# Raw rows from another queue, a schedule dated step by step, and 12 probability buffers

## The chip, the cores and the metric

The kernel runs on one core of a Trainium2 chip. The metric is the device time of one execution in microseconds (us), as the median of several runs. The engines are named as in the profile: PE (TensorE, matrix products; PEld is its loading of weights), ACT (ScalarE), DVE (VectorE), POOL (GpSimd) and SP (SyncE, which here only issues DMAs; SPq and POOLq are the issuing queues of SP and POOL).

## The reference

```python
# q, k, v: (4 batches, 8 heads, 768 rows, 64);  centroids: (8, 16, 64)
q_assign = argmax(einsum('bhsd,hcd->bhsc', q_n, c_n))     # q_n, k_n, c_n: rows over their lengths
k_assign = argmax(einsum('bhsd,hcd->bhsc', k_n, c_n))
scores = matmul(q, k.T) / sqrt(64), -1e9 where q_assign != k_assign
attn = softmax(scores);  x = (attn @ v) as (3072 tokens, 512)
h = x @ w_in                                              # w_in: 512 x 2048
out = (h * sigmoid(h)) @ w_out                            # w_out: 2048 x 512
```

A query attends only to the keys that fall to the same centroid; a gated layer of width 2048 follows.

## The kernel before

**The stages of one head.** A head is one of 32 pairs (batch, head), numbered 0 to 31; batch 1 begins at head 8, batch 2 at 16, batch 3 at 24. Its raw rows of q and k (`raw`, two DMAs of 192 KB, function `load`, L113) are split into a high and a low f16 half (`hi` L124, on DVE or ACT, and `lo` L137, on DVE; tile `hl`; together the split). One DMA transpose on SP's queue turns the halves (`xpose`, L144, tile `ab`). PE multiplies them with the centroids (`logits_1`, tile `psN`), DVE adds the parts, takes the maximum and compares (`lsum`, `mx_n`, `ge_n`, L197 to L227); the resulting one-hot code is brought into the rows of `ab` that the scores product reads. For batches 0 and 1 that takes a product and a copy (`cd_mm`, `cd_ev`), for batches 2 and 3 a scaling on POOL, a small DMA transpose on SP and a DMA from POOL (`c_scale`, `c_xpose` L239, `c_move` L243). With the codes in place, one scores product also applies the mask.

**Units.** Scores are made in 192 units (`qk_mm`, L352: two matmuls of 128x384), each followed by one exponential on ACT into a probability buffer (`exp`, L365, tile `P`). There are two score banks (`pS`), so scores u+2 wait for exponential u. Six units feed one value product (`pv`, L373), in up to three pieces in the listing; it needs the values of two heads (`load_v` L296, `cast_v` L301 on POOL). `norm` divides, and the result is turned into tile `xt` on PE or by a DMA transpose on SP.

**The gated layer.** A half batch has 16 hidden blocks (`unit_a_end`, L440, four matmuls of 128x384 with `win_s`), each followed by a tanh on ACT and a gate on DVE (L452, tile `gt`). The outputs follow either in plain parts of four matmuls (`part_b`, L464) or, from batch 1 on, in a `Pair` of two token tiles that needs seven products instead of eight (L519 to L599; its differences of weights, `tw`, lie in freed raw buffers). Results leave by DMAs from SP, the very last two by `c21_last` (L593). The weights come on POOL's queue (`w_load`, L601): `win_s` in eight pieces, `wout_s` in four quarters, the last two of them released after exponentials 22 and 23.

**What sets the order.** The first 27 units follow a listing written out by hand (`plan`, L777). Behind it a planner runs at build time: it keeps a clock for each engine, takes for each the piece whose estimated time has come, and writes the instructions in that order. Every engine executes its own list strictly in order. `date` (L853) attaches a step to a unit; `chain` (L858) plans a head's steps from split to codes; the loop at L922 dates loads, values, splits and casts by a formula in the head's number; `options` (L1133) ranks PE's candidates with the constants `PACE, LEAST, GAIN, HOLD` (L815). PE's four single banks are handed out by `bank`, and a piece waits at run time until the bank's last reader is done.

Of the kernel before, what the change touches and what calls it, by code (L numbers as in the profile page):

```python
# [34 lines left out]
def kernel(  # L35
# [74 lines left out]
    def raw_tag(n):  # L110
        return f"raw{n % 8 if n < EARLY else 5 + n % 3}"

    def load(job, eng=nc.sync):  # L113
        n = len(raws)
        raw = mp.tile([128, 12, D], f32, name="raw", tag=raw_tag(n), bufs=1)
        for dst, ap in job.srcs:
            o = raw[:, dst, :]
            if len(ap.shape) == 2:
                eng.dma_start(o.rearrange("p n d -> p (n d)"), ap)
            else:  # L120
                eng.dma_start(o.rearrange("p (h n) d -> p h (n d)", h=4), ap)
        raws[job.name] = raw
# [242 lines left out]
    def exp(u):  # L365
        P = mp.tile([128, 2, HALF], f16, name="P", bufs=16)
# [142 lines left out]
    cps = {}  # L509

    def keep(b, n):
        if b not in cps:
            cps[b] = [mp.tile([128, HK, 128], f16, name="cp", tag=f"ab{10 + m}", bufs=1) for m in range(2)]
# [5 lines left out]
    class Pair:  # L519
# [73 lines left out]
        def c21_last(self, part):  # L593
# [5 lines left out]
            nc.sync.dma_start(self.rows()[:, 0, x], self.ot2[:, x])  # L599
# [215 lines left out]
    PACE, LEAST, GAIN = 1.40, 17, .03  # L815
    HOLD = 6
    MARGIN = 0.3
    EARLY_T = 72


    moves_end = 11
# [34 lines left out]
    code_at, tensor_todo, after_unit = {}, [], {}  # L856

    def chain(job, b):  # L858
        def split(t):
            if job.name not in loaded:  # L860
                waiting[job.name] = split
                return
            t = max(t, loaded[job.name] + 0.4)
            either(t, 0.5, 0.72, lambda e: hi(job, "act" if e == "A" else None), lambda t: add("DVE", t, 0.9, lambda: lo(job), turned, 1.5), 1.5)

        def turned(t):
            u = last_use.get(place[job.name] - 12, 0)
# [4 lines left out]
            add("SP", t, 1.5, lambda: xpose(job), lambda t: tensor_todo.append((lands(t, 2.45) + (5.0 if b == 3 else 2.2 if b == 2 else 1.8), 0.35, lambda: logits_1(job), sums)), 0.0 if b == 1 else 3.0)  # L872
# [7 lines left out]
        def codes(t):  # L880
            if job.late:
                add("POOL", t, 0.8, lambda: c_scale(job), lambda t: add("SP", t, 1.33, lambda: c_xpose(job), moved))
# [3 lines left out]
        def moved(t):  # L886
            add("POOL", lands(t, 0.41) + 0.2, 0.6, lambda: c_move(job), lambda t: known(t + 0.7))
# [12 lines left out]
    loaded, waiting, values_at = {}, {}, {}  # L900
# [4 lines left out]

    def got(job, t):
        loaded[job.name] = lands(t - 0.25, 1.31)
        if job.name in waiting:
            waiting.pop(job.name)(t)

    def got_v(i, t):
        values_at[i] = lands(t + 0.5, 0.65)
# [3 lines left out]
    def cast(i, t):  # L916
        if i not in values_at:
            waiting[i] = lambda t: cast(i, t)
        else:
            add("POOL", max(t, values_at[i] + 0.4), 0.6, lambda: cast_v(i))  # L920

    for i in range(H, B * H):  # L922
        b, h = divmod(i, H)
        p = int((32 + 3.2 * h, 67+5.0*h, 106+5.2*h)[b - 1]) | 1
        job = jobs[i]
        if i > H + 3:
            date(max(FIRST, p - (8 + min(h, 4) if b == 1 else 16)), lambda t, job=job: add("SP", t, 1.05, lambda: load(job), lambda t: got(job, t), 3.0))
        if i >= H + 2:
            date(p - (6 if b == 1 else 9), lambda t, i=i, b=b: add("POOL", t, 0.6, lambda: load_v(i, nc.gpsimd), lambda t: got_v(i, t)) if b >= 2 else add("SP", t, 0.7, lambda: load_v(i), lambda t: got_v(i, t)))
        date(p - (3 if b == 1 else 6), chain(job, b))  # L930
        date(p, lambda t, i=i: cast(i, t))
# [27 lines left out]
    kinds = {(b, c): [0, 1, 2] for b in range(B) for c in range(2)}  # L959
    for b, c in kinds:  # L960
        if b >= 1:
            kinds[b, c] = ["p", 2]
        if b >= 2:
            kinds[b, c] = ["x", "p"] if c else ["p"]
# [9 lines left out]
    def norm_piece(n, t):  # L974
# [9 lines left out]
        def after(t):  # L984
            if by_dma(n):
                add("SP", t, 1.28, lambda: xn_d(i, c), lambda t: ready(lands(t, 0.61) + 1.5))
# [19 lines left out]
    def new_pair(b, c, kind):  # L1006
        key = b, c, kind
        at.setdefault(key, {})
        t = (1 if b >= 2 else 0) if kind == "p" and c else 0
        if kind == "x":  # L1010
            r2 = (lambda h: cps[b][h]) if b in cps else tokens(b, 0, NM - 1)
            pairs[key] = Pair(kind, b, tokens(b, 1, 0), r2, NM - 1, SG[kind])
        else:
            pairs[key] = Pair(kind, b, tokens(b, c, t + 1), tokens(b, c, t), c * NM + t, SG[kind], key == LAST)
# [10 lines left out]
        if not users[kind] or "over" in at[users[kind][-1]]:  # L1025
            tell(key, "turn", 0.0)
        users[kind].append(key)
        def over(t):
            add("DVE", t + 0.2, 0.69, pr.c12, sent)
            tell(key, "over", t)  # L1030
            n = users[kind].index(key) + 1
            if n < len(users[kind]):
                tell(users[kind][n], "turn", t)
# [4 lines left out]
        qb.extend((b, c, kind, k) for k in order)  # L1038

    def unit_piece():  # L1040
# [3 lines left out]
        def gated(t):  # L1044
            gate_at[b, c, fb] = t
            for h, name in enumerate(("lo", "hi")):
                need = [gate_at.get((b, c, x)) for x in range(h * HK, h * HK + HK)]
                if h == fb // HK and None not in need:
# [3 lines left out]
                    if (b, c) in ((2, 0), (3, 0)):  # L1052
                        old = b, 1, "x"
                        at.setdefault(old, {})
                        if b == 2:
                            add("SP", t, 0.7, lambda h=h: keep(b, h), lambda t, name=name: tell(old, name + "2", lands(t, 1.0) + 1.5))
                        else:
                            tell(old, name + "2", t)

        def then(t):  # L1060
# [7 lines left out]
            elif fb == NFB - 1 and kinds[b, c][0] == 0:  # L1068
                qb.extend((b, c, t_, n) for t_ in range(NM) for n in range(4))
# [63 lines left out]
    def options(t):  # L1133
# [3 lines left out]
        if unit < NU and unit - 2 in exp_at and 6 * pv_next > unit - 11:  # L1137
            i, c, m = units[unit]
            jn = {qc[i, c][0].name, kt[i, 2 * m][0].name}
            if all(j in code_at for j in jn):  # L1140
# [7 lines left out]
                mean, least = sum(works[max(x - 1, 0) : 7]) / len(works[max(x - 1, 0) : 7]), LEAST  # L1148
                if x < 3:
                    stock, mean, least = 1.302 * len(qa) + 0.863 * len(qb) + 20.8 * (x - released), 20.8, 12  # L1150
# [109 lines left out]
```

## Time and profile before

| | us |
|---|---|
| median of 3 runs | 301.1 |
| the runs | 299.5, 301.1, 301.17 |
| the profiled execution | 300.67 |
| its span, first to last instruction | 298.9 |
| PE's granted clock over the span | 1.000 |

| engine | busy us | share of the span |
|---|---|---|
| PE | 289.3 | 97% |
| DVE | 224.0 | 75% |
| ACT | 222.3 | 74% |
| POOL | 73.3 | 25% |

The span begins with the first and ends with the last instruction; the execution's own time is 1.8 us longer. All times within the profile count from the span's start. Matmuls are pipelined, so the duration of one matmul in a row is a latency: where a row groups several ("x4"), its length tells the pace. A bracket at the end of a row gives how long the engine stood idle before it and what ended that.

### The profile page before, as it was taken

Reading aid. Unit: us, or ns where it says so; the run is one execution under the profiler, and the core shown is the slowest. Engines: PE = TensorE matmul, PEld = TensorE weight load, DVE = VectorE, ACT = ScalarE, POOL = GpSimd, SP = SyncE. Lnnn points to the kernel's source line nnn. Section 1 sums busy time; section 2 is a strip of 40 time slices with the busy share of each in tenths; the row PEclk is TensorE's granted clock in tenths of the full one; section 3 lists DMA queues with packets and bytes.
Section 4 is the critical chain, followed back from the end, with each engine's and each line's share of the span. In section 5 each row is a group of like instructions: output and inputs, shape, how many; then the busy total and the mean of one; then the engine's idle time right before and its main releaser. Section 6 shows DMA issues by size and latency. Waiting matters only on the chain.

```text
span 298.9 us, 8222 instructions
## 1 busy us (share of the span) xinstructions
PE 289.3 (97%) x3281; PEld 204.2 (68%) x3281; DVE 224.0 (75%) x474; ACT 222.3 (74%) x369; POOL 73.3 (25%) x133
## 2 busy tenths in 40 slices
PE   7899989999999999999999999999999999999994
PEld 3786756566676566667766776668667777776784
DVE  5999558787998599997789759896584535568933
ACT  4899879665896689986788769896887769854410
POOL 2894900010140052545424234232000000000000
PEclk9999999999999999999999999999999999999999
DMA  6789999999897688878899989753300021110114
GB/s 207 226 176 207 196 246 220 160 266 270 190 180 192 172 179 205 182 197 185 202 189 230 182 197 228 173 98 74 99 15 16 25 74 27 36 37 0 37 35 140
DMA packets 77364, 44.61 MB, mean 149 GB/s; under 512 B 56304, under 2 KB 73232, under 8 KB 77328
## 3 DMA queue, kind: packets, MB, share of 16 engines
q1 hardware_dynamic: 72240, 35.68, 52.2%
q0 software_dynamic: 4800, 8.13, 14.2%
q8 instruction: 25, 0.41, 0.6%
q10 hardware_dynamic: 288, 0.30, 0.3%
q14 instruction: 11, 0.09, 0.1%
HBM read 27.30 MB, written 6.29 MB: 112 GB/s over the span
## 4 chain that ended last, share of the span: by engine, by line
PE 78%; DMA 11%; ACT 5%; DVE 2%; issue 1%; POOL 1%; SPq 0%; ACTq 0%
PE ph L429 22%; PE pS L362 16%; PE po L551 15%; PE pO L379 10%; PE po L469 8%; DMA wout_s<-in_moe_w_out_dram 7%; ACT P L367 4%; PE psN L188 3%; PE wide L429 3%; DMA ab<-cd 2%; DMA raw<-in_q_dram 1%; PE wide L551 1%; DVE hl L140 1%; POOL hl L133 1%; ACT cd L265 0%
## 5 line engine op out<-in xcount | busy, mean ns | idle before, releaser
L367 ACT ACTIVATE P<-pS 128x768 f16<-128x768 f32 x192 | 155.1, 819 | 36.2 <-PE pS L362 35.7
L362 PE MATMUL pS<-ab 128*128 128x384 f16 x384 | 92.7, 326 | 0.9 <-DMA ab<-cd 0.5
L429 PE MATMUL ph<-xt,win_s 128*128 128x384 f16 x464 | 89.6, 326 | 0.9 <-DVE gt L452 0.8
L452 DVE SCALAR_TENSOR_TENSOR gt<-tn,ph 128x384 f16<-128x384 f32 x116 | 62.2, 550 | 23.2 <-ACT tn L449 22.2
L429 PEld LDWEIGHTS <-win_s 128*128 128x128 f16 x512 | 48.9, 98 | 31.7 <-issue 1.4
L449 ACT ACTIVATE tn<-ph 128x384 f32<-128x384 f32 x116 | 57.5, 502 | 7.6 <-PE ph L429 5.1
L362 PEld LDWEIGHTS <-ab 128*128 128x128 f16 x384 | 34.7, 98 | 20.5 <-issue 1.2
L379 PEld LDWEIGHTS <-P 128*128 128x128 f16 x1152 | 39.9, 97 | 4.4
L379 PE MATMUL pO<-vt,P 128*128 128x65 f16 x1152 | 41.2, 193 | 0.0
L551 PEld LDWEIGHTS <-gt 128*128 128x128 f16 x312 | 29.5, 98 | 6.2 <-DVE gt L533 0.7
L140 DVE SCALAR_TENSOR_TENSOR hl<-raw,hl 128x768 f16<-128x768 f32 (+3 forms) x35 | 32.5, 930 | 1.2 <-ACT hl L131 0.6
L469 PE MATMUL po<-wout_s,gt 128*128 128x512 f16 x128 | 32.8, 379 | 0.2 <-DMA wout_s<-in_moe_w_out_dram 0.2
L303 POOL CAST vt<-vn 128x384 f16<-128x384 f32 x32 | 19.3, 604 | 48.1 <-DMA vn<-in_v_dram 40.3
L551 PE MATMUL po<-wout_s,gt 128*128 128x256 f16 x168 | 21.3, 273 | 0.1
L245 POOL DMA_DIRECT2D ab<-cdt x16 | 8.9, 559 | 50.0 <-PE pS L362 20.4
L188 PEld LDWEIGHTS <-ab 128*128 128x128 f16 x458 | 17.4, 97 | 4.2 <-DVE ab L174 0.3
L469 PEld LDWEIGHTS <-gt 128*128 128x128 f16 x128 | 12.0, 98 | 10.8 <-issue 0.4
L389 DVE RECIPROCAL zr<-pO 128x6 f32<-128x6 f32 x32 | 6.2, 194 | 17.3 <-PE pO L379 17.0
L391 DVE TENSOR_TENSOR xn<-pO,zr 128x384 f16<-128x384 f32 x32 | 17.8, 557 | 1.1
L188 PE MATMUL psN<-stk,ab 128*128 128x32 f16 (+1 forms) x458 | 18.6, 188 | 0.0
L200 DVE TENSOR_REDUCE L<-psN 128x192 f32<-128x384 f32 (+1 forms) x27 | 14.8, 549 | 3.5 <-PE psN L188 3.4
L232 POOL TENSOR_SCALAR od<-od 128x96 f16<-128x96 f16 x16 | 8.8, 548 | 33.1 <-DVE od L225 32.6
(106 smaller groups left out, 276.8 us busy)
## 6 DMA issues: line engine op xcount, KB each, us to landing
raw<-in_k_dram SPq DMA_DIRECT2D x31, 192.0 KB, 4.0
out_dram<-ot SPq DMA_DIRECT2D x23, 256.0 KB, 2.3
raw<-in_q_dram SPq DMA_DIRECT2D x24, 192.0 KB, 3.9
vn<-in_v_dram SPq DMA_DIRECT2D x16, 192.0 KB, 4.4
vn<-in_v_dram POOLq DMA_DIRECT2D x16, 192.0 KB, 4.0
win_s<-in_moe_w_in_dram POOLq DMA_DIRECT2D x8, 256.0 KB, 7.1
wout_s<-in_moe_w_out_dram POOLq DMA_DIRECT2D x4, 512.0 KB, 18.5
raw<-in_q_dram SPq DMA_DIRECT2D x2, 384.0 KB, 4.3
```

Source lines behind the costliest of these rows:

```text
L140: nc.vector.scalar_tensor_tensor(out=hl[:, s, 1, :], in0=raws[job.name][:, s, :], scalar=QS, in1=hl[:, s, 0, :], op0=ALU.mult, op1=ALU.sub ...
L188: nc.tensor.matmul(L[:, n % g, :, n // g], ab[:, i, :], stk[:, job.groups[i // 3][0], x : x + w], start=(x == 0), stop=(x + w == 2 * HC),)
L303: nc.gpsimd.tensor_copy(vt[:, :, 0:D], vns.pop(i))
L362: nc.tensor.matmul(pS[:, e, 0:HALF], abs_[kj.name][:, kn, :], rhs, start=True, stop=True)
L367: nc.scalar.activation(out=P, in_=pst.pop(u)[:, :, 0:HALF], func=AF.Exp, bias=0.0, scale=ESC)
L379: nc.tensor.matmul(o[:, (2 * t + h) * VW : (2 * t + h + 1) * VW], Ps[i + h, c, j // 2][:, j % 2, ts(t, 128)], vtb[(i + h) % 13][:, j, 0:VW ...
L391: nc.vector.tensor_tensor(out=xn, in0=ov[:, :, 0:D], in1=zr.unsqueeze(2).to_broadcast([128, 2 * NM, D]), op=ALU.mult)
L429: nc.tensor.matmul(ph[:, 0:HALF], win_s[:, r, ts(fb, 128)], xts[b, c][:, r, :], start=(r == 0), stop=(r == NR - 1))
L449: nc.scalar.activation(out=tn, in_=ph[:, 0:HALF], func=AF.Tanh, bias=0.0, scale=1.0)
L452: nc.vector.scalar_tensor_tensor(out=gt[:, fb, :], in0=tn, scalar=1.0, in1=ph[:, 0:HALF], op0=ALU.add, op1=ALU.mult)
L469: nc.tensor.matmul(po, gts[b, c][:, fc, ts(t, 128)], wout_s[:, fc, :], start=(fc == 0), stop=(fc == NFB - 1))
L551: nc.tensor.matmul(o, l[:, f, :], x[:, x0 : x0 + w], start=(f == 0 and k in begins), stop=(f == HK - 1), skip_group_check=True)
```

## The change

- Raw rows of batches 2 and 3 (heads 16 to 31, 32 DMAs) are asked for by GpSimd; those of batch 1 stay on SP.
- Splits, loads, values and casts no longer follow one formula: `SPLIT` lists the unit of each head's split, and `AHEAD`, `VALUES`, `CAST` set the others per batch. The planner now follows buffers as well: a load waits until the old rows of its buffer are split, a value load until its buffer is cast, a cast until the value product before it has been issued, a split until an older head has been turned.
- Raw buffers: from the 17th load on (before: from the 19th) three buffers rotate, and the buffer goes by the head's place in the list of jobs.
- `P` has 12 buffers instead of 16. The listing's order stays as it is, so exponentials whose buffer is still being read wait for its reader.
- The planner's constants and several of its estimated durations change; splits and copies go to ScalarE more often (`MARGIN`).
- The first of the two last stores is issued by ScalarE.
- `Pair` rooms, `kept` and `CROSS` write the planning of pairs more generally; which pairs are made stays the same.

```diff
     def raw_tag(n):
-        return f"raw{n % 8 if n < EARLY else 5 + n % 3}"
+        return f"raw{n % 8 if n < 2 * H else 5 + n % 3}"
...
-        n = len(raws)
-        raw = mp.tile([128, 12, D], f32, name="raw", tag=raw_tag(n), bufs=1)
+        raw = mp.tile([128, 12, D], f32, name="raw", tag=raw_tag(place[job.name]), bufs=1)
...
-        P = mp.tile([128, 2, HALF], f16, name="P", bufs=16)
+        P = mp.tile([128, 2, HALF], f16, name="P", bufs=12)
...
-            nc.sync.dma_start(self.rows()[:, 0, x], self.ot2[:, x])
+            (nc.sync if part else nc.scalar).dma_start(self.rows()[:, 0, x], self.ot2[:, x])
...
-    PACE, LEAST, GAIN = 1.40, 17, .03
-    HOLD = 6
-    MARGIN = 0.3
-    EARLY_T = 72
+    PACE, LEAST, LESS, GAIN = 1.49, 29, 9, 0.05
+    HOLD, ROUND, SIDE, LEAD = 10, 9, 4, 11
+    MARGIN = -0.3
+    EARLY_T = 66
...
         def split(t):
+            old = int(job.name[1:]) - (3 if int(job.name[1:]) >= H + 8 else 4)
+            if old >= H + 2 and old not in turn_at:
+                after_turn[old] = split
+                return
...
+    def raw_free(i, t):
+        old = max((m for m in range(i) if raw_tag(m + 2) == raw_tag(i + 2)), default=0)
+        if old >= H and old not in split_at:
+            after_split[old] = lambda t: raw_free(i, t)
+        else:
+            t = max(t, split_at.get(old, 0.0) + 0.06)
+            if i >= 2 * H:
+                add("POOL", t, 1.1, lambda: load(jobs[i], nc.gpsimd), lambda t: got(jobs[i], t), 3.0)
+            else:
+                add("SP", t, 1.4, lambda: load(jobs[i]), lambda t: got(jobs[i], t), 3.0)
...
+    SPLIT = [27, 27, 35, 38, 42, 45, 51, 52, 62, 65, 69, 71, 82, 83, 84, 86, 89, 106, 116, 122, 123, 129, 130, 134]
+    AHEAD, VALUES, CAST = [10, 5, 7], [5, 9, 12], [3, 2, 14]
...
-        p = int((32 + 3.2 * h, 67+5.0*h, 106+5.2*h)[b - 1]) | 1
+        p = SPLIT[i - H]
         job = jobs[i]
         if i > H + 3:
-            date(max(FIRST, p - (8 + min(h, 4) if b == 1 else 16)), lambda t, job=job: add("SP", t, 1.05, lambda: load(job), lambda t: got(job, t), 3.0))
+            date(p - AHEAD[b - 1], lambda t, i=i: raw_free(i, t))
         if i >= H + 2:
+            date(p - VALUES[b - 1], lambda t, i=i: value_free(i, t))
...
-        date(p - (3 if b == 1 else 6), chain(job, b))
-        date(p, lambda t, i=i: cast(i, t))
+        date(p, chain(job, b))
+        date(p + CAST[b - 1], lambda t, i=i: cast(i, t))
...
-            turn = (turn + 1) % 7
+            turn = (turn + 1) % ROUND
```

More of the change, by code (lines that the diff above doesn't have):

```diff
@@ L512, in keep @@
         if b not in cps:
-            cps[b] = [mp.tile([128, HK, 128], f16, name="cp", tag=f"ab{10 + m}", bufs=1) for m in range(2)]
+            cps[b] = [mp.tile([128, HK, 128], f16, name="cp", tag=f"ab{10 + m}" if b > 1 else f"cp{m}", bufs=1) for m in range(2)]
         nc.sync.dma_start(cps[b][n], gts[b, 0][:, n * HK : n * HK + HK, ts(NM - 1, 128)])
@@ L899 @@
             code_at[job.name] = 4.0 if job.name == "x1" else 0.0
-    loaded, waiting, values_at = {}, {}, {}
+    loaded, waiting, values_at, pv_at, after_pv = {}, {}, {}, {}, {}
+    for n in range(4):
+        pv_at[n] = 0.0
     for n in range(8, 12):
@@ L985, in after @@
             if by_dma(n):
-                add("SP", t, 1.28, lambda: xn_d(i, c), lambda t: ready(lands(t, 0.61) + 1.5))
+                add("SP", t, 1.45, lambda: xn_d(i, c), lambda t: ready(lands(t, 0.61) + 1.5))
             else:
@@ L1038, in new_pair, with kept @@
         qb.extend((b, c, kind, k) for k in order)
+    def kept(b, h, t):
+        old, name = (b, 1, "x"), ("lo2", "hi2")[h]
+        at.setdefault(old, {})
+        if b < B - 1:
+            add("SP", t, 1.36, lambda: keep(b, h), lambda t: tell(old, name, lands(t, 1.0) + 1.5))
+        else:
+            tell(old, name, t)
+    if 0 in CROSS:
+        kept(0, 0, 1.0)
     def unit_piece():
@@ L1051, in gated @@
                             tell(key, name + x, max(need))
[L1052 to L1058, printed above, removed]
+                    if c == 0 and b in CROSS:
+                        kept(b, h, t)
         def then(t):
```

94 lines of the change are left out of this document (63 added, 31 removed).

## The prediction

> **What bounds the kernel now.** I read the page first, then PE's busy time by stretches of 10 us, then the chain of waits, then the timeline at the few places where PE stands still.
>
> ```profile
> span 298.9 us, 8222 instructions
> PE 289.3 (97%) x3281; PEld 204.2 (68%) x3281; DVE 224.0 (75%) x474; ACT 222.3 (74%) x369; POOL 73.3 (25%) x133
> ```
>
> ```profile
> 40.00:50.00 10.00, 9.16 (x88) 5.84 (x86) 7.42 (x15) 8.84 (x17) 0.00 (x0) 1.00 1.18 239
> ...
> 70.00:80.00 10.00, 9.91 (x113) 6.44 (x111) 8.52 (x19) 6.70 (x14) 1.36 (x2) 1.00 0.96 223
> ...
> 110.00:120.00 10.00, 10.00 (x112) 6.73 (x111) 9.87 (x22) 9.48 (x18) 2.51 (x5) 1.00 0.93 216
> ...
> 230.00:240.00 10.00, 9.78 (x105) 7.47 (x103) 5.55 (x11) 7.61 (x13) 0.00 (x0) 1.00 0.13 38
> ...
> 290.00:300.00 10.00, 4.83 (x52) 4.10 (x49) 3.70 (x8) 0.28 (x1) 0.00 (x0) 0.96 0.31 107
> ```
>
> The first numbers of a row are its length and PE's busy time. From 60 us to the last matmul PE is idle for some 0.4 us in all, even at 110 us, where VectorE and ScalarE are both above 9.4 of 10. The changed kernel issues the same matmuls, so behind 60 us there is next to nothing to win. What idle time is left lies before 60 us and in the last 4 us.
>
> ```profile
> 35.93 22.30 DMA wout_s<-in_moe_w_out_dram
> 58.27 1.02 PE po L469 x4
> ...
> 80.36 0.65 PE ph L429 x4
> ...
> 84.72 1.10 PE pO L379 x36
> ```
>
> The chain of waits holds one long transfer. The last quarter of the second weight matrix, asked for at 35.93, lands 22.30 us later at 58.23, and the next link is the matmul that needs it. All PE work listed behind that matmul follows in one saturated run to the end. So the end is the landing plus the PE work listed behind it. The other rows give PE's pace: four matmuls over 384 columns take 0.65 us, so a scores unit (two of them) takes 0.33.
>
> ```profile
> 43.65 0.81 PE L429 MATMUL ph<-xt,win_s 128*128 128x384 f16 x4 [0.84 <-DVE gt L452]
> ...
> 57.69 0.33 PE L401 MATMUL px<-ident,xn 128*128 128x128 f16 x3
> 58.27 1.02 PE L469 MATMUL po<-wout_s,gt 128*128 128x512 f16 x4 [0.25 <-DMA wout_s<-in_moe_w_out_dram]
> ```
>
> PE's three transposes at 57.69 last about 0.17 (three of 128 columns), so PE is there at 57.86 and begins at 58.27: it waits 0.4. The stall at 43.65 waits for a bank of the listing's last hidden block. Both orders are the same up to there, so it stays.
>
> **12 probability buffers.** In the listing, exponential 18 now needs the buffer of unit 6, whose last reader is the third piece of the second value product. In PE's order that piece stands behind scores 19 and before scores 20.
>
> ```profile
> 27.78 0.50 PE L362 MATMUL pS<-ab 128*128 128x384 f16 x2 [0.54 <-DMA ab<-cd]
> ...
> 30.64 0.49 PE L362 MATMUL pS<-ab 128*128 128x384 f16 x2
> 30.96 0.53 PE L379 MATMUL pO<-vt,P 128*128 128x65 f16 x12
> 31.49 0.48 PE L362 MATMUL pS<-ab 128*128 128x384 f16 x2
> ...
> 33.24 0.49 PE L362 MATMUL pS<-ab 128*128 128x384 f16 x2 [0.20 <-ACT P L367]
> ```
>
> ```profile
> 30.63 0.81 ACT L367 ACTIVATE P<-pS 128x768 f16<-128x768 f32 x1
> ```
>
> ```profile
> 32.38 0.81 ACT L367 ACTIVATE P<-pS 128x768 f16<-128x768 f32 x1 [0.24 <-ACT P L367]
> ```
>
> Exponential 18 began at 30.63. Now it can begin at 30.96 + 0.53 = 31.49, 0.86 later, and scores 20 (two score banks) wait for its end. The slack of 0.24 before 32.38 is used up first, so about 0.6 us reach PE; exponential 12 waits similarly, ahead of the DMA wait of 0.54 us at 27.78, which takes it up. Bounds: 0, if all of it were taken up, and 0.9. What is queued behind the waiting exponential is ScalarE's queue; who waits is PE. In the new order one scores unit fewer stands ahead of the matmul that needs the last weights, so PE reaches it at 57.86 + 0.6 - 0.33 = 58.13. That is still before 58.23: the landing hides the cost, and if the landing came earlier the 0.6 would show. The unit is now behind the landing: +0.33.
>
> **Splits dated one by one.** The first two splits (heads 8 and 9) go from units 30 and 32 to 27. In the new order their halves follow the listing's eighth gate directly.
>
> ```profile
> 41.52 2.07 DVE L452 SCALAR_TENSOR_TENSOR gt<-tn,ph 128x384 f16<-128x384 f32 x4 [0.53 <-ACT tn L449]
> ...
> 46.57 0.55 DVE L135 TENSOR_SCALAR hl<-raw 128x768 f16<-128x768 f32 x1
> 47.16 0.96 DVE L140 SCALAR_TENSOR_TENSOR hl<-raw,hl 128x768 f16<-128x768 f32 x1
> ```
>
> ```profile
> 48.15 4.20 SPq L149 DMA_TRANSPOSE ab<-hl  x1
> ```
>
> The eighth gate ends at 43.59, with the 0.6 at 44.2. Two high halves (0.55 each) and a low half (0.96) end at about 46.2, so the first big transpose is asked for at 46.2, 2 us earlier than 48.15, and the second passes the raw rows of head 12 on SP's queue. Both run against the weights:
>
> ```profile
> 48.00:52.00 4.00, 4.00 (x50) 2.76 (x47) 3.87 (x10) 3.78 (x7) 0.00 (x0) 1.00 1.24 208
> 52.00:54.00 2.00, 2.00 (x16) 1.08 (x14) 1.83 (x4) 1.62 (x4) 0.00 (x0) 1.00 1.24 191
> 54.00:56.00 2.00, 2.00 (x43) 1.51 (x41) 1.85 (x5) 1.30 (x2) 0.00 (x0) 1.00 1.33 99
> 56.00:58.00 2.00, 2.00 (x13) 1.05 (x12) 1.40 (x2) 1.19 (x3) 0.00 (x0) 1.00 1.30 60
> ```
>
> The last two figures are the DMA engines' share and GB/s. The engines are full throughout, but from 52, when the transpose's 4.2 us of issue are over, what they move falls from 208 to 99 and 60. Moved 2 us earlier, the transpose meets 2 x 208 = 416 KB of weights that used to pass alone. Lower bound: 0, if engines that are full anyway finish both together as before. Upper bound: 416 KB at (99 + 60)/2 = 80 GB/s take 5.2 us instead of 2, so +3.2. I take +0.9, nearer the first: the two microseconds after 52 still moved 191. The weights then land at 59.1 and PE, there at 58.13, waits for them.
>
> [...]
>
> **Raw rows on GpSimd's queue.**
>
> ```profile
> raw<-in_q_dram SPq DMA_DIRECT2D x24, 192.0 KB, 3.9
> ...
> vn<-in_v_dram SPq DMA_DIRECT2D x16, 192.0 KB, 4.4
> vn<-in_v_dram POOLq DMA_DIRECT2D x16, 192.0 KB, 4.0
> ...
> ab<-cdt POOLq DMA_DIRECT2D x16, 48.0 KB, 3.0
> ```
>
> ```profile
> L298 POOL DMA_DIRECT2D vn<-in_v_dram x16 | 9.2, 576 | 0.0
> ```
>
> 32 DMAs of 192 KB leave SP. On GpSimd each costs 0.576 us of issue, 18.4 us in all for an engine that is 25% busy; values land as fast from either queue (4.0 and 4.4). SP's relief wins nothing by itself, since PE did not wait for SP behind 60 us. The raw rows are now asked for later, those of heads 14 and 15 also because they use other buffers: in the new order the least PE work between asking and splitting is 7 us (head 20: 21 matmuls of hidden blocks, 13 of scores, 12 short logits, one value product: 3.4 + 2.1 + 0.4 + 1.1), where it was 10 or more. A landing of 4 us fits; if it took over 7, VectorE would stand in order before that split, with gates and norms behind it. Moves of codes are queued behind these loads and casts; they were asked for 8 us and more of PE work ahead of their scores, against a landing of 3.0. Casts stand over 20 us of PE work ahead of their products. I cost these at nothing.
>
> VectorE hands five high halves, three code copies and three output copies to ScalarE: the row at 110 us shows that both can be above 9.4 with PE at 10.00. The pacing constants reorder PE's pieces and end the scores 12 us of PE work earlier; with PE full either way that gains at most the 0.4 us of idle left, and might cost about 1.5 at stalls that no row shows. I take -0.2.
>
> **The end.**
>
> ```profile
> 294.87 0.28 ACT L598 ACTIVATE ot<-po 128x128 f32<-128x128 f32 x1 [5.84 <-PE po L551]
> ```
>
> ```profile
> 295.18 0.29 DVE L596 COPY ot<-po 128x128 f32<-128x128 f32 x1 [0.72 <-ACT ot L598]
> ```
>
> ```profile
> 295.38 0.89 SPq L599 DMA_DIRECT2D out_dram<-ot  x2
> ```
>
> The first of the two last stores goes out from ScalarE. The second, ready at 295.47, no longer waits behind it: issued by 295.9 instead of 296.27, -0.35.
>
> **Sum.** The profiled execution took 300.67 us with a span of 298.9; the 1.8 around it stay. 300.67 + 0.9 (landing) + 0.33 (unit behind it) - 0.2 - 0.35 = 301.35, say 301.3. The median of the runs shown, 301.1, is 0.4 above that execution.
>
> **Rivals.** (1) Full engines finish weights and transposes together, no delay: 300.67 - 0.1 + 0.33 - 0.2 - 0.35 = 300.3; this is also about the best that it can do, since an earlier PE would only wait longer for the same landing. For it: the share was 1.24 and more throughout. Against: GB/s fell to 60. (2) Slower: the transposes hold the last weight quarter for the full 3.2 us, PE stands until 61.4, and the time is 303.7; it decides from a landing of 61. For it: the rows at 54 and 56 us. Against: 191 at 52. (3) Slower: loads from GpSimd are held up. The deciding point is the 7 us above; the longest landing of raw rows in this trace, 10.3 us in the crowded first 40 us, would hold VectorE 3 us at heads 20 and 23 and the banks would cover some 1 of each: +4, so 305.
>
> ```profile
> DMA to landing us min/median/max: 2.5/4.0/10.3
> ```
>
> [...]
>
> **Numbers.** 301.3 with 0.50 (its own range 300.6 to 302.8), (1) 0.27, (2) 0.13, (3) 0.10. A difference of 1% (3 us) is about what a measurement can tell from no change. Faster by that needs 298.1: more than all idle time that can go, 0.05. Slower needs 304.1: (3) and half of (2), 0.16. The rest, 0.79, is no change. The range takes in (1) and (2), with a little more for their unknown terms, and leaves out (3): up to 304.3, and down to 299.2, since single runs of the kernel before lie between 299.5 and 301.17.
>
> **What would show it.** PE's wait before the matmul at 58 us grows from 0.4 to about 1 and begins some 0.2 later; the first big transpose is issued near 46; exponential 18 begins right after the third piece of the value product; PE stays at 10.00 from 60 to 290; raw rows from GpSimd land in 4 to 5 us; the last stores overlap. Wrong would be: weights landing by 58.2 (rival 1), or rows below 9.8 for PE between 60 and 290 us.

## The result, and the profile after

| | before | after |
|---|---|---|
| median, us | 300.3 (4 runs, 299.4 to 301.2) | 310.3 (4 runs, 307.2 to 312.1) |
| the profiled execution, us | 300.67 | 310.47 |
| its span, us | 298.9 | 308.3 |
| PE's granted clock over the span | 1.000 | 0.987 |

The ratio is 1.030, with a 95% interval of 1.021 to 1.039: slower, by 6 us more than the upper end of the range. (Ratios here are formed without executions more than 1.5% above the fastest of their kernel, among them 312.1 here and 314.0 and 315.1 in experiment 9, so they can differ a little from the quotient of the medians.)

The page of the changed kernel, its span, engines, and two rows of the 40 slices (7.7 us each): PE's clock in tenths, and what the DMA engines moved.

```profile
span 308.3 us, 8281 instructions
PE 291.7 (95%) x3281; PEld 205.3 (67%) x3281; DVE 218.8 (71%) x462; ACT 227.7 (74%) x381; POOL 90.7 (29%) x165
...
PEclk9999999999996999999999999999999999999999
...
GB/s 207 248 166 218 203 247 188 218 228 250 214 125 146 62 259 179 217 156 234 190 182 239 79 243 215 197 91 53 49 15 83 15 13 76 7 70 1 36 34 136
```

PE's busy time grew by 2.4 us and the span by 9.4, so most of the loss is idle time. The 13th slice has a clock of 6, and slices 12 and 13 (85 to 100 us) moved 125 and 146 GB/s where the four slices before them moved over 200. The busy time by stretches of 10 us says the same (length, PE busy, ..., clock, DMA share, GB/s):

```profile
70.00:80.00 10.00, 9.94 (x113) 6.59 (x112) 7.76 (x17) 8.27 (x15) 3.56 (x6) 1.00 1.00 223
80.00:90.00 10.00, 8.11 (x91) 5.30 (x88) 8.63 (x19) 8.57 (x16) 5.59 (x13) 1.00 1.13 167
90.00:100.00 10.00, 5.57 (x32) 3.20 (x33) 2.52 (x5) 2.96 (x5) 0.00 (x0) 0.66 1.06 151
```

The timeline of PE there, and the link of the chain of waits that ends at its first row:

```profile
94.43 0.82 PE L187 MATMUL psN<-stk,ab 128*128 128x32 f16 x12 [6.32 <-DMA ab<-hl]
...
95.92 2.77 PE L428 MATMUL ph<-xt,win_s 128*128 128x384 f16 x8
```

```profile
80.44 13.95 DMA ab<-hl
```

PE stands still for 6.32 us: the logits of a head wait for its big transpose, asked for at 80.44 and landed 13.95 us later. Counted in the order of the transposes this is head 14. (The expectations quoted below call it head 15, and they count some waits from a slightly different point: 1.12 us for the 0.96 and 0.66 for the 0.50 below.) In the kernel before the same transpose landed in 3.9 us. The second row is the clock: the last row of eight such matmuls ahead of the stall, at 86.32, lasts 1.46 us, this one 2.77.

What ran beside that transpose is in GpSimd's and SP's rows:

```profile
77.99 1.13 POOL L302 CAST vt<-vn 128x384 f16<-128x384 f32 x2 [6.12 <-DMA vn<-in_v_dram]
79.16 0.55 POOL L297 DMA_DIRECT2D vn<-in_v_dram  x1
79.75 0.54 POOL L118 DMA_DIRECT2D raw<-in_q_dram  x1
80.28 0.54 POOL L118 DMA_DIRECT2D raw<-in_k_dram  x1
80.83 0.54 POOL L118 DMA_DIRECT2D raw<-in_q_dram  x1
81.35 0.54 POOL L118 DMA_DIRECT2D raw<-in_k_dram  x1
81.88 0.54 POOL L297 DMA_DIRECT2D vn<-in_v_dram  x1
...
83.17 0.54 POOL L297 DMA_DIRECT2D vn<-in_v_dram  x1
```

```profile
80.44 2.26 SPq L148 DMA_TRANSPOSE ab<-hl  x1
...
86.44 8.30 SPq L148 DMA_TRANSPOSE ab<-hl  x1
```

GpSimd stood 6.12 us at a cast whose values had not landed; everything queued behind the cast, seven loads of 192 KB, then left within 4.6 us, around the moment when head 14's transpose was asked for. Two more followed at 86.47. The next big transpose took SP 8.30 us merely to issue.

The other places where PE now stands, in the listing and in the tail, are the releaser brackets of these rows of PE (and ScalarE's row for the first):

```profile
32.24 0.48 PE L361 MATMUL pS<-ab 128*128 128x384 f16 x2 [0.96 <-ACT P L366]
...
272.27 1.03 PE L550 MATMUL po<-wout_s,gt 128*128 128x256 f16 x8 [0.50 <-DVE ot L576]
280.31 1.03 PE L550 MATMUL wide<-tw,sg 128*128 128x256 f16 x8 [0.71 <-DVE gt L451]
293.87 0.38 PE L550 MATMUL wide<-tw,sg 128*128 128x256 f16 x2 [0.32 <-ACT ot L556]
```

```profile
31.38 2.96 ACT L366 ACTIVATE P<-pS 128x768 f16<-128x768 f32 x4 [1.00 <-PE pO L378]
```

**The 9.8 us between the two profiled executions** are 9.4 of span and 0.4 outside it. Of the span, the rows show these terms. The wait for the transpose: +6.32. The clock behind it: in the stretch from 91.80 to 98.63 (row below) PE is busy for 4.20 us at a clock of 0.50, which is worth half of that, +2.1. The tail, 0.50 + 0.71 + 0.32 = +1.53, where before PE stood at 10.00 in every stretch from 260 to 290. The probability buffers, 0.96 instead of 0.20 at that place, +0.76. The wait for the last weights, 0.25 before, is gone, -0.25. From the end of the last matmuls to the end of the span it is 3.71 us instead of 4.06, -0.35. And two waits of before in the first 10 us, 0.65 at 7.51 and 0.28 at 9.03, are missing in this execution, -0.9; they vary between executions (in experiment 1, the same order on PE, the first is back with 0.60). Sum 9.2; some 0.2 was not traced.

```profile
91.80:98.63 6.83, 4.20 (x25) 2.52 (x26) 1.97 (x4) 1.77 (x3) 0.00 (x0) 0.50 1.10 155
```

### The profile page after: what moved, and what is told of

It reads as the page before. It is cut to its first block, busy times and chain, and to the rows that moved or that the text cites. A ratio compares the mean times of both kernels' runs of the same rounds, so it can differ in the third digit from the quotient of the medians.

```text
span 308.3 us, 8281 instructions
## 1 busy us (share of the span) xinstructions
PE 291.7 (95%) x3281; PEld 205.3 (67%) x3281; DVE 218.8 (71%) x462; ACT 227.7 (74%) x381; POOL 90.7 (29%) x165
## 4 chain that ended last, share of the span: by engine, by line
PE 80%; DMA 9%; ACT 4%; DVE 3%; SPq 2%; issue 1%; POOL 1%; POOLq 0%; ACTq 0%; DVEq 0%
PE ph L428 21%; PE pS L361 18%; PE po L550 11%; PE pO L378 10%; PE po L468 9%; DMA ab<-hl 5%; PE wide L550 4%; PE wide L428 3%; PE psN L187 3%; DMA ab<-cd 2%; ACT P L366 2%; SPq L118 2%; DMA raw<-in_q_dram 1%; DVE gt L451 1%; DMA vn<-in_v_dram 1%
## 5 line engine op out<-in xcount | busy, mean ns | idle before, releaser
L361 PE MATMUL pS<-ab 128*128 128x384 f16 x384 | 93.7, 327 | 1.8 <-ACT P L366 1.0
L451 DVE SCALAR_TENSOR_TENSOR gt<-tn,ph 128x384 f16<-128x384 f32 x114 | 61.5, 551 | 32.5 <-ACT tn L448 31.9
L428 PEld LDWEIGHTS <-win_s 128*128 128x128 f16 x512 | 49.7, 99 | 32.8 <-issue 2.6
L361 PEld LDWEIGHTS <-ab 128*128 128x128 f16 x384 | 34.8, 98 | 21.3 <-issue 2.0
L378 PE MATMUL pO<-vt,P 128*128 128x65 f16 x1116 | 40.0, 193 | 0.0
L302 POOL CAST vt<-vn 128x384 f16<-128x384 f32 x32 | 20.5, 651 | 40.8 <-DMA vn<-in_v_dram 40.7
L550 PE MATMUL po<-wout_s,gt 128*128 128x256 f16 x144 | 18.5, 273 | 0.5 <-DVE ot L576 0.5
L468 PEld LDWEIGHTS <-gt 128*128 128x128 f16 x128 | 11.9, 98 | 10.3
L118 POOL DMA_DIRECT2D raw<-in_q_dram x16 | 9.3, 580 | 25.1 <-DVE hl L139 22.4
(117 smaller groups left out, 304.5 us busy)
```

The lines of the kernel that those rows point to most:

```text
L302: nc.gpsimd.tensor_copy(vt[:, :, 0:D], vns.pop(i))
L361: nc.tensor.matmul(pS[:, e, 0:HALF], abs_[kj.name][:, kn, :], rhs, start=True, stop=True)
L378: nc.tensor.matmul(o[:, (2 * t + h) * VW : (2 * t + h + 1) * VW], Ps[i + h, c, j // 2][:, j % 2, ts(t, 128)], vtb[(i + h) % 13][:, j, 0:VW ...
L428: nc.tensor.matmul(ph[:, 0:HALF], win_s[:, r, ts(fb, 128)], xts[b, c][:, r, :], start=(r == 0), stop=(r == NR - 1))
L451: nc.vector.scalar_tensor_tensor(out=gt[:, fb, :], in0=tn, scalar=1.0, in1=ph[:, 0:HALF], op0=ALU.add, op1=ALU.mult)
L468: nc.tensor.matmul(po, gts[b, c][:, fc, ts(t, 128)], wout_s[:, fc, :], start=(fc == 0), stop=(fc == NFB - 1))
```

## The experiments

**1. The raw rows on SP again.** In the changed kernel only the issuing engine is put back; the order on PE, VectorE and ScalarE is identical.

```diff
-                add("POOL", t, 1.1, lambda: load(jobs[i], nc.gpsimd), lambda t: got(jobs[i], t), 3.0)
+                add("POOL", t, 1.1, lambda: load(jobs[i], nc.sync), lambda t: got(jobs[i], t), 3.0)
```

> The changed kernel with one thing undone: the raw rows of heads 16 to 31 leave from SP again, at the same places of the order; the order on PE, VectorE and ScalarE is that of the changed kernel. Theory A (the burst of 192-KB loads from GpSimd between 79 and 87 us shares the DMA engines by turns with SP's big transposes and stretches them): the stall of 6.3 us before head 15's logits at 87.6 us goes, and with it the lower clock behind it; 310.3 - 6.4 - 2 = 302, within 301 to 303, and the transposes asked for between 75 and 90 us land in under 8 us. Rival B (the new dates put the transposes of heads 14 to 16 too close behind each other and to their use): the stall stays at 5 to 6.5 us, 308 to 310. Rival C (the engines are simply full, whoever asks): the loads now stand ahead of the transposes in SP's own queue, the stall shrinks to 2 to 5 us, 304 to 308.

304.6 us (302.0 to 305.6), ratio to the kernel before 1.013 (1.006 to 1.020): over half of the loss is gone, but the median is above theory A's 301 to 303. In the profiled execution (301.96, the fastest of the four) the stall and the lower clock are gone, and the transpose lands in 5.1 us. PE, clock and DMA engines in three stretches of 4 us, first of the changed kernel, then of this one:

```profile
82.00:86.00 4.00, 4.00 (x68) 2.99 (x64) 3.74 (x9) 3.77 (x7) 2.21 (x6) 1.00 1.02 148
86.00:90.00 4.00, 2.11 (x13) 1.07 (x11) 2.90 (x7) 2.91 (x6) 1.38 (x3) 1.00 1.29 108
90.00:94.00 4.00, 0.00 (x0) 0.00 (x0) 0.00 (x0) 0.00 (x0) 0.00 (x0) 0.73 1.14 176
```

```profile
82.00:86.00 4.00, 4.00 (x67) 3.05 (x66) 3.74 (x10) 3.72 (x7) 2.42 (x5) 1.00 0.91 225
86.00:90.00 4.00, 4.00 (x38) 2.58 (x36) 3.97 (x9) 3.90 (x9) 0.69 (x2) 1.00 0.91 195
90.00:94.00 4.00, 4.00 (x55) 2.74 (x54) 2.38 (x7) 3.15 (x6) 0.00 (x0) 1.00 1.13 246
```

The engines are full in both kernels (share 0.9 to 1.3), but in the changed one they move 108 to 176 GB/s, in this one 195 to 246. GpSimd's queue from 80 to 94 us (packets, MB, share of the 16 engines' time that the packets took), in the same order:

```profile
q0 software_dynamic: 461, 1.44, 69.4%
```

```profile
q0 software_dynamic: 384, 1.18, 26.8%
```

Per byte its packets took over twice as long in the changed kernel (48% per MB against 23), so a share above 1 is not engines at their best: it counts the time that packets were under way. SP's rows of this run show why the transpose was spared:

```profile
80.83 1.89 SPq L148 DMA_TRANSPOSE ab<-hl  x1
...
87.35 2.59 SPq L148 DMA_TRANSPOSE ab<-hl  x1
90.00 0.58 SPq L118 DMA_DIRECT2D raw<-in_q_dram  x1
```

In one queue the raw rows of head 16 stand behind the transposes and leave at 90.00, ten microseconds later than from GpSimd, and nobody misses them. So the edit changed both the queue and the moment at which the loads leave. Rival B (dates) falls, since the dates are the same and the stall is gone. Rival C was not put to the test, though 304.6 lies in its range, since the loads did not stand ahead of the transpose as it assumed. Single executions came out up to 3.6 us above the profiled one, which theory A did not say.

**2. The kernel before with its raw rows on GpSimd**, nothing else.

```diff
-add("SP", t, 1.05, lambda: load(job), lambda t: got(job, t), 3.0)
+add("SP", t, 1.05, lambda: load(job, nc.gpsimd if i >= 2 * H else nc.sync), lambda t: got(job, t), 3.0)
```

> The kernel before with one part of the change alone: the raw rows of heads 16 to 31 are issued by GpSimd at the same places of the order, all dates as they were. Theory A: the transposes issued beside them land later than the 5.0 us median of before, and where a head's logits have little spare time PE stands; 1 to 8 us slower, 301.5 to 308. Rival B (the dates are the cause): GpSimd's loads cost nothing by themselves, 300 to 301.

308.6 us, ratio 1.024 (1.018 to 1.031): this part alone makes most of the loss. It falls mainly at another head: head 16's transpose, 3.8 us in the kernel before, lands in 10.3, with three loads from GpSimd between 95.9 and 97.0 us beside it. (Three shorter waits for transposes, 0.27 to 0.87 us, come at other heads. Head 14's, with six loads from GpSimd within 4 us of it, lands in 5.8 us, and PE does not wait.) PE's row, and the DMA engines from 100 to 104 us, first here, then in the kernel before:

```profile
107.03 0.82 PE L188 MATMUL psN<-stk,ab 128*128 128x32 f16 x12 [3.80 <-DMA ab<-hl]
```

```profile
100.00:104.00 4.00, 3.23 (x32) 1.64 (x28) 2.87 (x5) 2.64 (x4) 0.00 (x0) 1.00 1.21 96
```

```profile
100.00:104.00 4.00, 4.00 (x43) 2.31 (x40) 3.37 (x6) 2.58 (x4) 0.00 (x0) 1.00 0.64 181
```

**3. Sixteen probability buffers** in the changed kernel (`bufs=12` back to `bufs=16`).

> The changed kernel with 16 probability buffers again, nothing else. If exponential 18 waiting for the third piece of the second value product is what holds PE 1.12 us at 30.9 us, that stall falls to 0.2 to 0.4 and the time by 0.6 to 0.9, unless the weights for the matmul at 58 us then land after PE gets there, in which case the gain is lost there again. The rival, that the stall at 30.9 comes from the score banks or the listing: unchanged. The stall of 6.3 us at 87.6 stays in either case, give or take 1 us.

```profile
33.82 0.48 PE L361 MATMUL pS<-ab 128*128 128x384 f16 x2 [0.20 <-ACT P L366]
...
59.19 1.02 PE L468 MATMUL po<-wout_s,gt 128*128 128x512 f16 x4 [0.92 <-DMA wout_s<-in_moe_w_out_dram]
...
98.74 0.82 PE L187 MATMUL psN<-stk,ab 128*128 128x32 f16 x12 [5.71 <-DMA ab<-hl]
```

The wait in the listing goes from 0.96 back to 0.20, as expected. PE then waits 0.92 for the last weights, which took 22.65 us here: the cover that the prediction named is real when the landing is late. The single execution took 315.67, because the transposes were worse still: head 14's landed in 15.7 us, and a code 2.48 us late just ahead of it.

**4 and 5. The price by itself.** The kernel before, with three extra loads beside the transposes of heads 18 to 21, once from GpSimd and once from SP.

```diff
     def xpose(job, part=None):
...
+        if job.name in ("h18", "h19", "h20", "h21"):
+            nc.gpsimd.tensor_copy(pace, hl[0:1, 11, 1, 0:1])
+            for n in range(3):
+                o = mp.tile([128, 6, D], f32, name="more", tag=f"more{n}", bufs=1)
+                nc.gpsimd.dma_start(o.rearrange("p n d -> p (n d)"), nat(k, 0, 0, 6))
```

(In the other kernel the last line reads `nc.sync.dma_start`; both have 13 probability buffers.)

> A measurement of the disputed price by itself: the kernel before, with three more loads of 192 KB (nothing reads them) asked for by GpSimd at the moment when the halves of heads 18 to 21 are ready, that is together with their big transpose on SP (and 13 probability buffers, for the room). In the kernel before these transposes land in 2.2 to 5.0 us, median 4.1. Theory A (two queues on one DMA engine cost more than the sum of their loads): the four transposes land in 9 us or more, and the loads too. Rival C (the engines are shared without loss: three loads are 576 KB, at the 200 GB/s and more of the undisturbed stretches 2.8 us): 5 to 8 us. PE stands where the spare time of a head's logits is used up.

> The same kernel with the same twelve loads at the same places, only asked for by SP, ahead of each transpose in its own queue. Theory A: the transposes wait for the loads and no more; from the ask for the first load to the landing of the transpose some 7 us, and no stretch in which full engines move under 150 GB/s. Rival C: the same 7 us here, and no difference to the kernel in which GpSimd asks; 300 to 303 for both.

| from the first ask (load or transpose) to the landing of the transpose, us | head 18 | 19 | 20 | 21 |
|---|---|---|---|---|
| the kernel before, no extra loads | 5.0 | 4.2 | 4.4 | 5.7 |
| loads from GpSimd | 8.3 | 6.9 | 8.0 | 11.6 |
| loads from SP, ahead of the transpose | 8.8 | 8.0 | 7.3 | 8.3 |

The single executions took 306.17 us (GpSimd) and 309.06 us (SP), both above rival C's 300 to 303 and above the 302.45 of the kernel before, so loads ahead of the transposes in SP's queue are no bargain either. Theory A in its strict form falls: three loads cost a transpose about the same whichever queue they come from, three times in four. The fourth time (asked for at 131.18, loads at 132.10) it took 11.6. Nor did the rates keep to it, which on SP were to stay at 150 GB/s or more: with the loads on SP the stretches of 4 us from 110 to 142 moved 137 to 354 (137 from 114, at a share of 1.12), with the loads on GpSimd those from 116 to 144 moved 117 to 309 (168 from 128 at 1.21, 117 from 136 at 1.00). Both queues at once cost more than one (11.6 us against 8.3 at head 21), but did not at head 19 (6.9 against 8.0).

**6. Values on SP too.** Experiment 1 with the value loads of batches 2 and 3 on SP (`load_v(i)` for `load_v(i, nc.gpsimd)`), so that GpSimd asks for codes alone.

> The changed kernel with the raw rows of heads 16 to 31 on SP as in the run with that alone (304.6, single executions 302.0 to 305.6), and the value loads of batches 2 and 3 on SP as well, so that GpSimd asks only for codes. Theory A: what is left in that run and moves from execution to execution is the value loads meeting transposes; 301 to 302.5 with a spread under 2 us. Rival B (the rest is the order: pacing, dates, 12 buffers): 303 to 305 as before, or worse where SP is now late.

303.6 us over 10 executions (301.5 to 304.5); the kernel before ran at 302.45 beside it, ratio 1.003 (1.000 to 1.007). Head 14's transpose lands in 4.0 us. The interval reaches down to 1. But theory A's 301 to 302.5 was missed, the spread of 3.0 us is wider than it said, and 303.6 lies in rival B's range: this profile has some 2.3 us more of waits that belong to the order than the kernel before (0.97 instead of 0.20 at the buffers' place, 1.54 in the tail).

**7. The old pacing constants** in experiment 1.

```diff
-    PACE, LEAST, LESS, GAIN = 1.49, 29, 9, 0.05
-    HOLD, ROUND, SIDE, LEAD = 10, 9, 4, 11
+    PACE, LEAST, LESS, GAIN = 1.40, 17, 9, 0.03
+    HOLD, ROUND, SIDE, LEAD = 6, 7, 4, 11
```

> The changed kernel with the raw rows on SP and with the pacing constants of the kernel before (PACE, LEAST, GAIN, HOLD, ROUND). The stalls of 0.66, 0.88 and 0.49 us before pair products at 263, 271 and 285 us are put down to the scores ending 12 us earlier, which leaves pair products waiting for VectorE at the end: with the old constants they go, and 304.6 becomes 302 to 303. Rival: they come from something else, and the time stays within 1 us of 304.6; the dates of splits were chosen for the new pace, so new stalls may also appear in 60 to 200 us, 305 to 310.

307.2 us, ratio 1.017 (1.009 to 1.025). PE by stretches of the tail, and its longest wait elsewhere:

```profile
270.00:280.00 10.00, 9.53 (x72) 6.73 (x71) 7.89 (x16) 5.37 (x12) 0.00 (x0) 1.00 0.00 1
280.00:290.00 10.00, 10.00 (x76) 7.30 (x75) 8.03 (x16) 4.64 (x11) 0.00 (x0) 1.00 0.08 28
```

```profile
57.66 1.02 PE L468 MATMUL po<-wout_s,gt 128*128 128x512 f16 x4 [2.35 <-DMA wout_s<-in_moe_w_out_dram]
```

The tail's waits fall from 1.53 to about 0.5, which speaks for the pace as their cause. But PE now reaches the last weights earlier and waits 2.35 there, and other waits open up to 116 us: dates and pace were set for each other, and this run can't price one without the other.

**8 and 9. Where the loss lies.** Of the changed kernel's raw rows, only those of heads 16 to 18 go back to SP (`nc.sync if i < 19 else nc.gpsimd`), and then only those of heads 19 to 31.

> The changed kernel with the raw rows of heads 16 to 18 alone, the six loads asked for between 79 and 87 us, issued by SP again; those of heads 19 to 31 stay with GpSimd. The theory as it now stands, D: with seven loads asked for by GpSimd within 5 us, head 15's transpose has to share the DMA engines with all of them, where one queue would have served it first in order; the cost lies at that one place. Then the stall of 6.3 us at 87.6 is gone and the time is that of the run with all raw rows on SP, 302 to 305.6. Rival: GpSimd's loads cost wherever they are; the time falls by less than half, 306 to 309, with stalls of 1 us and more before logits behind 100 us.

> The complement: heads 16 to 18 from GpSimd as in the changed kernel, heads 19 to 31 from SP. D: the whole loss stays, a stall of 4 to 8 us before 95 us and 308 to 312. Rival: 304 to 307, the loss is spread over all of them.

The first: 305.6 us, ratio 1.013 (1.007 to 1.018), the same as with all raw rows on SP. The second: 306.9 to 315.1 us, ratio 1.022 (1.014 to 1.031). The 26 loads of heads 19 to 31 cost nothing that can be seen; the six of heads 16 to 18 bring the loss back, by the ratio not quite to the changed kernel's 1.030, though the intervals overlap. PE's wait at head 14, in the first and in the second:

```profile
90.45 0.52 PE L187 MATMUL psN<-stk,ab 128*128 128x32 f16 x12 [2.60 <-DMA ab<-hl]
```

```profile
91.76 0.57 PE L187 MATMUL psN<-stk,ab 128*128 128x32 f16 x12 [3.63 <-DMA ab<-hl]
```

In the first the stall is not gone, as D had it, but 2.60 us: three value loads from GpSimd are still there. In the second it is 3.63 us, a little under D's 4 to 8.

**10. The burst taken apart.** All raw rows stay on GpSimd; only the casts of batch 1 are dated later, which changes GpSimd's order alone.

```diff
-    AHEAD, VALUES, CAST = [10, 5, 7], [5, 9, 12], [3, 2, 14]
+    AHEAD, VALUES, CAST = [10, 5, 7], [5, 9, 12], [8, 2, 14]
```

> The changed kernel with the casts of batch 1 dated 8 units behind the split instead of 3; only GpSimd's order changes: the value loads and the raw rows of head 16 now stand ahead of the two casts on which GpSimd waited 6.1 us until 78 us, the raw rows of head 17 behind them. All raw rows stay on GpSimd. D (the burst comes from GpSimd standing at a cast, its loads queued behind it): the loads go out in two groups, the first some 6 us earlier, and the stall at 87.6 falls to 0 to 3 us, 303 to 307. Rival (the transpose of head 15 is late whatever GpSimd asks for and when, or the earlier group now meets the transpose before it): the stall stays at 5 us or more, or one as long appears within 15 us of it; 308 to 312.

305.3 us, ratio 1.013 (1.007 to 1.019). GpSimd's rows:

```profile
72.19 1.44 POOL L297 DMA_DIRECT2D vn<-in_v_dram  x2
73.67 0.54 POOL L118 DMA_DIRECT2D raw<-in_q_dram  x1
74.20 0.54 POOL L118 DMA_DIRECT2D raw<-in_k_dram  x1
81.02 0.97 POOL L302 CAST vt<-vn 128x384 f16<-128x384 f32 x2 [6.29 <-DMA vn<-in_v_dram]
```

Four loads leave before the cast, four behind it, and head 14's transpose lands in 7.6 us, at 90.77, just ahead of its use at 90.82; PE has no wait there (this execution has one of 2.13 us at 39 us, for a code in the listing, ahead of all that the edit touches). So at this head it was not GpSimd's queue as such, but what had piled up behind one waiting cast. At head 16 of experiment 2 three loads were enough.

The profiled executions around head 14 side by side, value loads counted too. "Room" is 7.5 us, from the ask (80.83) to the use (88.33) in experiment 1, where PE never waited. (Experiments 2, 4, 5 and 12 have the order of before; the extra loads of 4 and 5 come only at head 18.)

| kernel | loads asked for by GpSimd within 4 us of the transpose | landing, us | PE's wait for it, us |
|---|---|---|---|
| experiment 6 | 0 | 4.0 | none |
| experiment 11 | 0 | 6.5 | none |
| before | 2 | 3.9 | none |
| experiment 12 | 2 | 3.8 | none |
| experiment 4 | 2 | 3.7 | none |
| experiment 5 | 2 | 8.4 | 1.54 |
| experiment 1 | 3 | 5.1 | none |
| experiment 7 | 3 | 8.05 | 0.78 |
| experiment 8 | 3 | 10.1 | 2.60 |
| experiment 10 | 4 | 7.6 | none |
| experiment 2 | 6 | 5.8 | none |
| experiment 9 | 7 | 11.1 | 3.63 |
| after | 7 | 13.95 | 6.32 |
| experiment 3 | 7 | 15.7 | 5.71 |

With seven it was late in three executions of three; with two to six in three of nine, with none in neither of two. So a burst makes a late transpose likely and long, but the count alone does not decide: six loads passed in experiment 2, two did not in experiment 5. This may also be where the spread of experiment 1 comes from; its slower executions have no profile.

**11. A candidate**: experiment 6 with 16 probability buffers.

> The kernel with raw rows and values of batches 2 and 3 on SP (303.6; before on the same chip 302.45) with 16 probability buffers. If the stall of 1.14 us at 31 us is the twelve buffers', it falls to 0.2 to 0.4 and the time by 0.6 to 0.9, 302.7 to 303; if PE then only waits longer for the last weights at 58 us, 303.3 to 303.8. Faster than the kernel before it would be only if the tail's 2.2 us of stalls went too, which nothing here changes.

```profile
33.12 0.48 PE L361 MATMUL pS<-ab 128*128 128x384 f16 x2 [0.22 <-ACT P L366]
...
57.98 1.02 PE L468 MATMUL po<-wout_s,gt 128*128 128x512 f16 x4 [0.41 <-DMA wout_s<-in_moe_w_out_dram]
```

303.5 us over 10 executions, ratio 1.009 (1.006 to 1.012). The 0.75 us gained in the listing is half lost again at the weights, and the time is that of experiment 6. The kernel before ran at 300.8 beside it, not 302.45, so experiment 6's 1.003 is no proof that nothing of the loss is left.

**12. The last store alone**: the kernel before, with the first of the two last stores issued by ScalarE.

> The kernel before with one part of the change alone: the first of the two last stores is issued by ScalarE. The term of the prediction for it was -0.35 us: the time from the start of the last matmuls (294.56 in the profile of before, span 298.9, so 4.34) falls to about 4.0, and the median by 0.1%, which the timing can hardly tell from nothing. Rival: the store from ScalarE takes longer to land than the one from SP and ends last itself; no gain, or up to 0.5 us more.

301.4 us beside 302.0, ratio 0.997 (0.993 to 1.001): not told from nothing. The last store was issued 0.4 us earlier, but lands in 2.0 us where it took 1.6 before, and from the end of the last matmuls to the end of the span it is 4.05 us against 4.06, as the rival said. No version here is shown to beat the kernel before.

## Why the prediction was wrong

**What bounds the kernel** was read rightly: in the changed kernel too, away from three places PE was above 9.9 in every stretch of 10 us, and nearly all that was lost is idle time or clock of PE. Both signs that the prediction named for being wrong came: the weights landed at 57.3, before 58.2, and rows of PE fell to 8.11 and 5.57.

**Raw rows on GpSimd's queue is the step that failed**: "I cost these at nothing." It measured 6.3 us and 2.1 of clock behind it; experiments 1, 8, 9 and 2 put that on this edit. Three parts of the step were wrong.

- It asked whether the moved loads would be in time ("A landing of 4 us fits; if it took over 7, VectorE would stand"). Their medians, 4.6 and 5.2 us, fit. In the burst they took up to 12.2 us, and nobody waited for them. What was late was the transfer that they ran beside. The room of head 14's transpose, 7.5 us against a landing of 4, was never worked out.
- It took GpSimd at 25% busy as an engine that issues a load when it is due. It issued them when what stood before them in its order was done: the value loads' cast held it for 6.12 us, and the seven loads behind it came out within 4.6 us. Experiment 10 moved the cast and the stall was gone, with no room to spare.
- It dismissed SP's queue as relief without worth ("PE did not wait for SP behind 60 us"). SP's order had been worth something: in one queue the loads stood behind the transposes. (Ahead of them, as in experiment 5, they cost as much as from GpSimd.)

Rival (3) had loads from GpSimd as the danger, but as loads held up, with VectorE standing at heads 20 and 23 and a price of 4 us. The place was head 14 and the engine that stood was PE. A reason to give it more than 0.10 stood in the prediction: the rows at 54 to 58 us, where a transpose and the weights from GpSimd together moved 99 and 60 GB/s, were used for the price of the weights alone, and not for the 32 loads that were to meet transposes from then on.

For the size of the step, an estimate from these runs: with raw rows on SP the engines moved 195 to 246 GB/s here (experiment 1, 82 to 94 us). If all seven loads, 1.38 MB, went through before the transpose was done, they would add some 6.5 us at 210 GB/s to the 3.9 of its landing in the kernel before, 10.4 in all. Experiment 9 with 11.1 is near that; 13.95 and 15.7 are over it, in executions whose engines moved less (from 82 to 94 us a mean of 144 GB/s in the changed kernel and 169 in experiment 3, against 183 in experiment 9); six loads in experiment 2, with 5.8, are well under it. From 80 to 94 us in the changed kernel 461 packets of GpSimd's queue ran beside 2351 of SP's; in what order the engines took them was not shown.

**12 probability buffers.** Right in mechanism: exponential 18 waited 1.00 us for the value product, and PE 0.96 instead of 0.20, +0.76 where 0.6 was told. It was not hidden in the profiled execution, where the last weights landed at 57.3 (asked for at 36.4, 20.9 us) and nobody waited; in experiment 3, with a landing of 22.65, taking the buffers' wait away only lengthened the wait for weights.

**Splits dated earlier.** The first big transpose was asked for at 45.87 (46.2 was told). The +0.9 for the weights isn't seen: the last quarter took 20.5 to 22.65 us in the eight executions with the early splits (mean 21.3; after and experiments 1, 3, 6 to 9, 11) and 19.3 to 22.6 in the five with the late ones (mean 20.9; before and experiments 2, 4, 5, 12). Executions differ by more than the term; rival (1)'s assumption fits as well.

**Pacing**, -0.2: wrong in sign, +1.53 in the tail. The prediction had named about 1.5 as what it might cost, and set it aside. It argued that no row shows a stall there; with the scores over 12 us earlier, what is left at the end is hidden blocks and pair products, and PE waits for VectorE and ScalarE between them. That it goes with the constants is supported by experiment 7, though nothing else stayed equal there.

**The end**, -0.35: right in size by luck. The last store was issued earlier, but it landed 2.62 us after the end of the last matmuls, against 2.66 before. The other 0.3 lies behind that landing, where the closing steps of the program take 1.10 us instead of 1.39; no run shows why, and alone (experiment 12, 2.62 and 1.43) the store brought nothing.

## What to carry to other kernels

Before a transfer is moved to another queue, work out the room of the transfers that it will then run beside, not only its own: one queue was also a rule of precedence (in experiment 1 the raw rows of head 16 left SP at 90.00, behind the transposes). An idle engine is no free issuer if its list has waits in it, so look for what stands before the moved DMAs and count how many leave at once when that wait ends (here seven, behind a wait of 6.12 us). And where a saturated engine stands for several microseconds, add the clock that it comes back with (here 0.50 for 6.83 us behind a stall of 6.32, worth 2.1).

## What was not expected of the hardware

Full DMA engines moved as little as half in some stretches. With loads from GpSimd and big transposes from SP at once, stretches at a share of 1.0 to 1.3 moved 96 to 176 GB/s (after, experiment 2), against 195 to 246 at the place of the former with the raw rows on SP (experiment 1). With the extra loads on SP a stretch moved 137 at 1.12 (experiment 5). It comes and goes: three loads beside a transpose gave landings of 5.1 and 10.1 us in experiments 1 and 8, and 6.9 and 11.6 in experiment 4. What decides it was not found; a larger burst from each queue in turn was not tried.

The clock fell after shorter pauses than the 6.32 us of the changed kernel, too. In experiment 8 PE stood for 2.60 us, and half the clock followed:

```profile
87.83:91.24 3.41, 0.81 (x17) 0.69 (x17) 1.04 (x3) 1.02 (x3) 0.00 (x0) 1.00 1.31 146
91.24:94.65 3.41, 3.41 (x13) 1.62 (x11) 1.79 (x5) 2.07 (x4) 0.00 (x0) 0.50 0.77 225
```

Over all the traces here the clock changes only at the ends of stretches of 3.41 us, counted from its first rise. It fell behind each stretch at full clock in which PE was busy for 0.32 of the time or less (after, experiments 2, 3, 4, 8, 9; the pauses were 2.47 to 6.32 us) and behind none with 0.58 or more (the lowest, in experiment 7, holds most of the pause of 2.35 us). So where a pause lies counts as well as how long it is. Half the clock then lasted 3.41 us, or 6.83 (after) and 13.65 (experiment 3). The 6.32 us of the changed kernel hold a whole such stretch in which PE was busy for 0.00 us (88.39 to 91.80); the pauses of 2.47 to 2.60 us are shorter than one, and in experiment 8 the stretch with 0.81 us of PE work was enough.
